# Gated linear attention and a feed-forward layer on one core: chunk ends of three units by another way, clears on VectorE, and a new order of all engines

## The chip, the cores and the metric

The kernel runs on one core of a Trainium2 chip. The metric is device time in microseconds (us) of one execution, as a median over several runs; the profile is one further execution of the same program, with its own time.

## What is computed

Two stages. The first is a gated linear attention, per batch (4) and head (8), over 768 positions with 48 elements a head; the second is a feed-forward layer on its output, 384 to 2048 and back, with a leaky ReLU.

```python
f = 1.0 / (1.0 + np.exp(-f_logit))
state = np.zeros((B, H, D, D), dtype=np.float32)
for t in range(S):
    state = f[:, :, t, :, None] * state + np.einsum('bhd,bhe->bhde', k[:, :, t], v[:, :, t])
    y[:, :, t] = np.einsum('bhd,bhde->bhe', q[:, :, t], state)
...
x = np.ascontiguousarray(attn_out.transpose(0, 2, 1, 3)).reshape(B * S, H * D)
h = x @ w_in
g = np.maximum(0.01 * h, h)
return (g @ w_out).astype(np.float32)
```

Inputs and output are float32; the matmuls take bfloat16.

## The kernel before

**Units.** The positions are cut into chunks of 128. A unit is 256 rows of work (L40). Units 0 to 3 ("paired") are the first two chunks of one batch each; units 4 to 11 are one later chunk (2 to 5) of two batches each. In the words below, the first number is the unit; the second is a half of it (heads 0 to 3 or 4 to 7 of a paired unit, or a chunk or batch), with 2 for both.

**The order** is written out by hand: a string of words (L583), each calling one small function, so that every engine gets its instructions in the order of the words that concern it (the schedule is manual, L53). A word is name_unit_arguments@banks, the banks being PSUM banks of 512 columns. All engines run their own words in sequence; semaphores tie them. SyncE issues all DMAs from one queue, in order, and an issue that has to wait for a buffer holds up those behind it.

**The words of the attention.** Lf, Lk, Lq, Lv load f_logit, k, q, v of a unit (L153; five buffers each). ge and gl (L233, L237) are ScalarE's exponential and logarithm of the gate. cs (L249) sums the logarithms along the chunk on TensorE by a triangular matrix, L264, and for units 4 to 9 also gives the sum over the whole chunk per element, in four narrow matmuls with a column of ones, L267. dec (L273) makes the decays on ScalarE: em (L275), at (L276), and from L267's columns the decay at the chunk's end, end (L281). k and q (L289, work at L293) multiply keys and queries with them; the last number chooses VectorE (0) or GpSimd (1). tk, tq turn both by TensorE in units 0 to 3 (L326), and ck, cq copy the result out of PSUM (VectorE 0, ScalarE 1); xk, xq turn them by a DMA in units 4 to 11 (L346). sc is the scores on TensorE (L362, L369), mk their mask on VectorE (L379, L383), mx their product with the values plus the old state's share (L400), ms the state's share in paired units. xt copies the result to bfloat16 (VectorE 0, ScalarE 1). v (cast_v, L296) casts the values on GpSimd. pt (L464) is the state's new part on TensorE, sf (L481) adds it on VectorE, and sb (state_end, L492) multiplies the state by end and casts it, on GpSimd.

**The words of the feed-forward.** up (L500) makes 256 of the 2048 columns for a unit in six matmuls (L506), pr (L509) is ScalarE's leaky ReLU of them (L511), dn (L513) a quarter of a down-projection in four matmuls (L518), dh a half of the last one by columns (L540). ob and oh copy the output out of PSUM, st and sh store it. WI_0 to WI_4 load w_in in pieces of 384, 384, 768, 768 and 768 KB, WO_0 to WO_3 w_out in pieces of 768 KB; the 768 KB pieces share a ring of three buffers, so that WO_0 needs WI_2's buffer, and WO_3 WO_0's. cw (L186) casts half a piece: cw_0 for w_in, cw_1 for w_out; the last number is VectorE (0), ScalarE (1) or GpSimd (2). up_j_2 and up_j_3 need both halves of WI_2, up_j_4 and 5 those of WI_3, up_j_6 and 7 those of WI_4.

**The filler.** id_n (L202) runs matmuls of 128 n columns on a tile of ones, into a bank that nobody reads then; it computes nothing and lies where TensorE has no work. The order before has 12 of them, 106 blocks of 128 columns, all ahead of unit 2's sums.

**At the start** VectorE clears tiles (L82 to L90) and builds a mask (L114, L116), and L119 clears the eight tiles of the cast states, two on VectorE and six on GpSimd.

## Time and profile before

| | us |
|---|---|
| median of 3 runs | 179.62 (179.17 to 179.93) |
| profiled execution | 179.25 |
| its span, first to last record | 177.4 |

The profile's page gives, for the span: how long each engine was busy and with how many instructions; the span cut into 40 slices; the DMA queues; the chain of work that ended last; and groups of instructions by line, with their busy time, the mean length of one, and the idle time just before them with what ended it. PE is TensorE's matmuls, PEld its weight loads, DVE is VectorE, ACT ScalarE, POOL GpSimd, SP SyncE, and SPq SyncE's issue of DMAs. The granted TensorE clock is a mean of 1.00 over the span. A timeline's row gives start, length, engine, line and operands, and in square brackets the idle time ahead of it. Records of matmuls overlap, since they are pipelined: the time that one costs is read from the distance of two starts.

### The profile page before, as it was taken

To read this page: it belongs to the slowest core of one execution; us is meant where nothing else is said; L and a number is where in the kernel's file an instruction comes from. 1 tells how busy PE (TensorE), PEld (TensorE's weight loads), DVE (VectorE), ACT (ScalarE), POOL (GpSimd) and SP (SyncE) were. 2 spreads that over 40 slices of the span, in tenths; PEclk is the share of its full clock that TensorE was granted. 3 is DMA by queue.
4 is the path that set the end of the run, shared out by engine and by line. 5 is a ranking of instruction groups with operands and counts; after the bars stand their busy time and mean duration, and the time that the engine had idled before them with its cause. 6 is when DMAs were issued, how large, how long until landed. Compare 5 with 4: busy or idle time off the path is not lost.

```text
span 177.4 us, 5625 instructions
## 1 busy us (share of the span) xinstructions
PE 170.6 (96%) x2318; PEld 129.4 (73%) x2318; DVE 83.5 (47%) x164; ACT 114.3 (64%) x236; POOL 64.2 (36%) x137
## 2 busy tenths in 40 slices
PE   7698999999999999999999999999999999999992
...
GB/s 144 283 289 326 358 353 362 364 344 199 221 206 202 222 222 206 185 250 193 234 125 202 182 229 127 235 162 203 172 217 262 0 70 140 89 4 0 48 44 89
DMA packets 106473, 34.44 MB, mean 194 GB/s; under 512 B 100688, under 2 KB 104656, under 8 KB 106448
## 3 DMA queue, kind: packets, MB, share of 16 engines
...
q14 instruction: 7, 0.06, 0.1%
...
## 4 chain that ended last, share of the span: by engine, by line
PE 90%; ACT 3%; DVE 3%; DMA 1%; issue 1%; DVEq 0%
PE ps L506 36%; PE ps L518 35%; PE ps L400 6%; PE ps L369 2%; PE ps L326 2%; DVE qh L293 2%; PE ps L264 2%; PE ps L540 1%; DMA f_raw<-in_f_logit_dram 1%; PE ps L478 1%; DVE wm L379 1%; PE ps L362 1%; PE ps L206 1%; PE ps L473 1%; ACT at L276 1%
## 5 line engine op out<-in xcount | busy, mean ns | idle before, releaser
L511 ACT ACTIVATE gT<-ps 128x512 bf16<-128x512 f32 x96 | 56.2, 620 | 28.7 <-PE ps L506 27.1
L506 PE MATMUL ps<-xT,w_in 128*128 128x256 bf16 x576 | 71.4, 273 | 0.0
L518 PE MATMUL ps<-w_out,gT 128*128 128x384 bf16 x368 | 68.8, 326 | 0.0
L506 PEld LDWEIGHTS <-w_in 128*128 128x128 bf16 x576 | 59.9, 110 | 5.6 <-ACT w_in L198 0.4
L518 PEld LDWEIGHTS <-gT 128*128 128x128 bf16 x368 | 34.2, 98 | 18.7
L495 POOL TENSOR_TENSOR sf<-sf,end 128x192 f32<-128x192 f32 x16 | 9.1, 570 | 40.7 <-DVE sf L490 34.5
L383 DVE TENSOR_TENSOR wm<-ps,ut 128x512 bf16<-128x512 f32 x32 | 19.9, 683 | 8.3 <-PE ps L369 6.5
L564 DVE COPY osb<-ps 128x384 f32<-128x384 f32 x13 | 7.2, 556 | 26.5 <-PE ps L518 20.6
L498 POOL CAST sb<-sf 64x192 bf16<-64x192 f32 x40 | 13.6, 341 | 10.3 <-DVE sf L488 8.0
L293 DVE TENSOR_TENSOR kh<-k_raw,em 128x768 bf16<-128x768 f32 (+1 forms) x10 | 8.5, 853 | 18.6 <-ACT em L275 18.5
L490 DVE TENSOR_TENSOR sf<-sf,ps 64x192 f32<-64x192 f32 x32 | 11.2, 350 | 12.2 <-issue 5.1
L460 ACT CAST xT<-ps 128x384 bf16<-128x384 f32 x14 | 6.9, 513 | 12.7 <-PE ps L400 12.6
L275 ACT ACTIVATE em<-ps 128x384 bf16<-128x384 f32 x24 | 12.1, 503 | 4.2 <-DVE sf L490 2.9
L298 POOL CAST vb<-v_raw 128x384 bf16<-128x384 f32 (+1 forms) x16 | 11.7, 731 | 8.2 <-PE ps L400 5.0
L462 DVE CAST xT<-ps 128x384 bf16<-128x384 f32 x10 | 5.6, 571 | 15.5 <-PE ps L400 15.5
L276 ACT ACTIVATE at<-ps 128x384 bf16<-128x384 f32 x24 | 12.2, 509 | 0.0
L235 ACT ACTIVATE f_raw<-f_raw 128x384 f32<-128x384 f32 (+1 forms) x16 | 10.7, 679 | 1.8 <-DMA f_raw<-in_f_logit_dram 1.8
L379 DVE TENSOR_TENSOR wm<-ps,pair_mask 128x512 bf16<-128x512 f32 x16 | 10.1, 684 | 2.9 <-PE ps L362 2.9
L247 ACT ACTIVATE lf<-f_raw 128x384 bf16<-128x384 f32 (+1 forms) x16 | 10.7, 682 | 0.3
L206 PE MATMUL ps<-warm 128*128 128x512 bf16 (+3 forms) x30 | 9.2, 413 | 1.1 <-DVE warm L82 1.1
L293 POOL TENSOR_TENSOR kh<-k_raw,em 128x384 bf16<-128x384 f32 (+1 forms) x6 | 6.9, 1161 | 8.4 <-DMA q_raw<-in_q_dram 4.4
L293 DVE TENSOR_TENSOR qh<-q_raw,at 128x384 bf16<-128x384 f32 (+1 forms) x11 | 9.3, 857 | 0.0
...
## 6 DMA issues: line engine op xcount, KB each, us to landing
...
ring<-in_moe_w_out_dram SPq DMA_DIRECT2D x4, 768.0 KB, 6.6
...
ring<-in_moe_w_in_dram SPq DMA_DIRECT2D x3, 768.0 KB, 9.1
v_raw<-in_v_dram SPq DMA_DIRECT2D x4, 384.0 KB, 6.4
```

The lines of the kernel that those rows point to most:

```text
L206: nc.tensor.matmul(banks[bank][:, 0:128 * m], warm, warm[:, None, :].to_broadcast([128, m, 128]), start=True, stop=True)
L275: nc.scalar.activation(ems[j % 2][:, a], t[:, 0:H * D], AF.Exp, scale=1.0)
L276: nc.scalar.activation(ats[j % 2][:, a], t[:, 0:H * D], AF.Exp, scale=-1.0)
L293: eng.tensor_mul(heads(j, to[j % NR], a)[:, :, :, 0:D], raw_heads(j, x, a), decays(j, by, a))
L298: nc.gpsimd.tensor_copy(out=heads(j, vb, a), in_=raw_heads(j, "v", a))
L379: nc.vector.tensor_mul(w.rearrange("t (s p) n -> t s p n", s=2), src.rearrange("t (s p n) -> t s p n", s=2, p=2), pair_mask[:, :, None, :] ...
L383: nc.vector.tensor_mul(w, src.rearrange("t (p n) -> t p n", p=P2), ut[:, None, :].to_broadcast([128, P2, 128]))
L490: nc.vector.tensor_add(sf[rows], sf[rows], new)
L498: nc.gpsimd.tensor_copy(out=sb[rows, :, y * D:y * D + D], in_=sf[rows])
L506: nc.tensor.matmul(pm[:, i, :], w_in_of(ff, kk), xTs[j % 3][:, kk].rearrange("t a s -> t (a s)"), start=(kk == 0), stop=(kk == NK - 1))
L511: nc.scalar.activation(gTs[j % 3][:, 2 * g:2 * g + 2, :], pm, AF.Prelu, alpha=0.01)
L518: nc.tensor.matmul(po, gTs[j % 3][:, ff, 128 * a:128 * a + 128], w_out_b[quarter][:, ff % 4, :], start=(ff == 0), stop=(ff == NF - 1))
```

## The change

Four things. Units 5, 7 and 9 (ED) no longer sum whole chunks in L267's matmuls. Instead ScalarE takes, in dec, an exponential of the last 32 rows of the running sums (384 columns) into a new tile, lasts, and the word ed sends its last row to the tile end in two small DMAs from SyncE. VectorE clears all eight tiles of the cast states, and the four tiles end. cast_v can run on ScalarE and state_end on VectorE, by a last number in the word. And the order of all engines is written anew; it has 12 fillers of 112 blocks. The diff, with the orders cut:

```diff
--- before.py
+++ after.py
@@ -58,14 +58,15 @@
         return [const.tile(shape, dtype, name=f"{name}{i}", tag=f"{name}{i}") for i in range(n)]
     NR, NB = 3, 5
-    ED = ()
+    ED = (5, 7, 9)
     raws = {x: tiles(NB, [128, 2, H, D], FP32, x + "_raw") for x in "fkqv"}
     lfs = tiles(NR, [128, 2, H, 64], BF16, "lf")
     khs = tiles(NR, [128, 2, H, 64], BF16, "kh")
     qhs = tiles(NR, [128, 2, H, 64], BF16, "qh")
     ems = tiles(2, [128, 2, H * D], BF16, "em")
-    ats = tiles(2, [128, 2, H * D], FP32 if ED else BF16, "at")
+    ats = tiles(2, [128, 2, H * D], BF16, "at")
     ends = tiles(4, [128, 2, P2], FP32, "end")
+    lasts = tiles(2, [128, 2 * H * D], FP32, "last")
     vbs = tiles(3, [128, 2, H, D], BF16, "vb")
     v2s = tiles(3, [128, 2 * P2, 4, 16], BF16, "v2")
     kTs = tiles(2, [128, 2 * P2, 128], BF16, "kT")
@@ -83,9 +84,6 @@
     for i in range(NR):
         for t in (lfs[i], khs[i], qhs[i]):
             nc.vector.memset(t[:, :, :, D:64], 0.0)
-    if ED:
-        for t in ends:
-            nc.vector.memset(t, 0.0)
     for t in v2s:
         nc.vector.memset(t[:, :, 1:3, :], 0.0)
@@ -116,7 +114,10 @@
         nc.vector.tensor_copy(out=pair_mask[rows, 1, 0:64], in_=bs[rows, rows])
     for b in range(B):
         for t in sbs[b]:
-            (nc.vector if b == 0 else nc.gpsimd).memset(t, 0.0)
+            nc.vector.memset(t, 0.0)
+    if ED:
+        for t in ends:
+            nc.vector.memset(t, 0.0)
     ut = const.tile([128, 128], BF16, tag="ut")
     make_upper_triangular(nc, ut, val=1.0, diag=True)
@@ -277,14 +278,21 @@
         if paired(j):
             nc.scalar.activation(end_of(j)[:, :, 2 * a:2 * a + 2].rearrange("t i p -> t p i"),
                                  t[:, 384:388].rearrange("t (p i) -> t p i", i=2), AF.Exp, scale=-1.0)
-        elif chunk(j, a) < NCH - 1 and j not in ED:
+        elif j in ED:
+            nc.scalar.activation(by_element(j)[C - 32:C, P2 * a:P2 * a + P2],
+                                 t[C - 32:C, 0:H * D].rearrange("t (p y d) -> t p y d", y=2, d=D), AF.Exp, scale=-1.0)
+        elif chunk(j, a) < NCH - 1:
             nc.scalar.activation(end_of(j)[:, a], t[:, H * D:H * D + P2], AF.Exp, scale=-1.0)
+    def by_element(j):
+
+        return lasts[j % 2].rearrange("t (y d g) -> t g y d", y=2, d=D)
+
     def end_dma(j):
+        row = lasts[j % 2][C - 1:C].rearrange("o (y d g) -> o y d g", y=2, d=D)
         for y in range(2):
-            src = ats[j % 2][127:128].rearrange("o a (p y d) -> o y d (a p)", y=2, d=D)[:, y]
-            nc.sync.dma_start(out=end_of(j)[64 * y:64 * y + D].rearrange("d a p -> d (a p)"), in_=src)
+            nc.sync.dma_start(out=end_of(j)[64 * y:64 * y + D].rearrange("d a p -> d (a p)"), in_=row[:, y])
     def scale(x):
         def go(j, a, e):
@@ -293,18 +301,19 @@
             eng.tensor_mul(heads(j, to[j % NR], a)[:, :, :, 0:D], raw_heads(j, x, a), decays(j, by, a))
         return go
-    def cast_v(j, a):
+    def cast_v(j, a, e=0):
         vb, v2 = vbs[j % 3], v2s[j % 3]
-        nc.gpsimd.tensor_copy(out=heads(j, vb, a), in_=raw_heads(j, "v", a))
+        copy = nc.scalar.copy if e else nc.gpsimd.tensor_copy
+        copy(out=heads(j, vb, a), in_=raw_heads(j, "v", a))
         if paired(j):
             p = slice(0, P2) if a == 2 else slice(2 * a, 2 * a + 2)
             src = by_pair(raw(j, "v")).rearrange("t (p j) s d -> t j s p d", j=2)
             dst = v2.rearrange("t (s p) n e -> t n s p e", s=2)
             for i in range(2):
-                nc.gpsimd.tensor_copy(out=dst[:, 3 * i, :, p], in_=src[:, i, :, p, 32 - 32 * i:48 - 32 * i])
+                copy(out=dst[:, 3 * i, :, p], in_=src[:, i, :, p, 32 - 32 * i:48 - 32 * i])
         else:
             a2 = slice(a, a + 1) if a < 2 else slice(0, 2)
-            nc.gpsimd.tensor_copy(out=v2[:, P2 * a2.start:P2 * a2.stop, 0:4:3, :],
+            copy(out=v2[:, P2 * a2.start:P2 * a2.stop, 0:4:3, :],
                                   in_=raw(j, "v")[:, a2].rearrange("t a (p j) d -> t (a p) (j d)", j=2)[:, :, 32:64]
                                   .rearrange("t p (j e) -> t p j e", j=2))
@@ -489,13 +498,14 @@
             else:
                 nc.vector.tensor_add(sf[rows], sf[rows], new)
-    def state_end(j, a):
+    def state_end(j, a, e=0):
+        eng = nc.vector if e else nc.gpsimd
         sf, sb = sfs[batch(j, a)], sbs[batch(j, a)][chunk(j, a) % 2]
         if chunk(j, a) > 0:
-            nc.gpsimd.tensor_mul(sf, sf, end_of(j)[:, a, :, None].to_broadcast([128, P2, D]))
+            eng.tensor_mul(sf, sf, end_of(j)[:, a, :, None].to_broadcast([128, P2, D]))
         for y in range(2):
             rows = slice(64 * y, 64 * y + 64)
-            nc.gpsimd.tensor_copy(out=sb[rows, :, y * D:y * D + D], in_=sf[rows])
+            eng.tensor_copy(out=sb[rows, :, y * D:y * D + D], in_=sf[rows])
     def up(j, g, bank):
         st[j]["pm", g] = bank
@@ -581,69 +591,70 @@
 
     order = """
-    Lf_0_0 Lf_0_1 Lk_0_0 Lk_0_1 Lq_0_0 Lq_0_1 ge_0_0 Lv_0_2 gl_0_0 Lf_1_2 ge_0_1 id_31@6 cs_0_0@0 Lk_1_2 gl_0_1
-    Lq_1_2 cs_0_1@1 dec_0_0 WI_0 k_0_0_0 Lv_1_2 dec_0_1 id_4@6 tk_0_0@2 WI_1 q_0_0_0 k_0_1_1 ck_0_0_1 WI_2
-    id_7@6 tq_0_0@3 q_0_1_0 cq_0_0_0 id_4@6 tk_0_1@4 tq_0_1@5 ck_0_1_1 sc_0_0@6.7 Lf_2_2 v_0_0 cq_0_1_1 mk_0_0_0
-    v_0_1 id_8@2 sc_0_1@0.1 mk_0_0_1 mk_0_1_0 id_7@4 pt_0_2@2.3 WI_3 ge_1_0 mk_0_1_1 ge_1_1 gl_1_0 sf_0_0 id_6@6
-    mx_0_2@4.5 gl_1_1 Lk_2_2 cs_1_0@6 sb_0_0 xt_0_0_1 cs_1_1@7 dec_1_0 sf_0_1 ms_0 k_1_0_1 xt_0_1_0 dec_1_1 WI_4
-    q_1_0_0 k_1_1_1 id_13@1 tk_1_0@0 q_1_1_0 tq_1_0@1 Lq_2_2 cw_0_0_1 ck_1_0_0 sb_0_1 id_3@3 tq_1_1@2 tk_1_1@4
-    cq_1_0_1 up_0_0@3 ck_1_1_0 cq_1_1_1 Lv_2_2 sc_1_0@6.5 v_1_0 pr_0_0 sc_1_1@7.0 mk_1_0_0 cw_0_1_1 v_1_1
-    mk_1_1_0 id_14@2 up_0_1@1 mk_1_1_1 mk_1_0_1 pt_1_2@4.2 pr_0_1 cw_0_3_2 sf_1_0 mx_1_2@3.6 cw_0_2_1 sb_1_0
-    xt_1_0_1 WO_0 id_4@0 up_0_2@7 ge_2_0 ge_2_1 sf_1_1 ms_1 up_0_3@0 pr_0_2 xt_1_1_0 sb_1_1 gl_2_1 up_1_0@5
-    gl_2_0 cw_0_5_1 up_1_2@1 cw_0_4_2 pr_1_0 pr_0_3 WO_1 id_5@3 cs_2_0@4 pr_1_2 cs_2_1@3 dec_2_0 up_1_4@2
-    k_2_0_1 up_1_1@7 dec_2_1 k_2_1_1 up_0_5@6 cw_0_6_0 pr_1_4 tk_2_0@5 pr_1_1 up_0_4@0 cw_0_7_0 pr_0_5 q_2_1_1
-    tk_2_1@1 pr_0_4 up_1_5@4 ck_2_0_0 WO_2 q_2_0_0 up_1_7@3 Lf_3_2 v_2_0 pr_1_5 ck_2_1_0 Lk_3_2 tq_2_0@2 pr_1_7
-    tq_2_1@7 v_2_1 cq_2_0_0 up_0_6@6 cq_2_1_0 sc_2_0@5.0 pr_0_6 cw_1_1_2 sc_2_1@1.4 mk_2_0_0 pt_2_2@3.2 cw_1_0_1
-    ...
-    pr_11_0 up_11_4@3 ob_10_1_0 up_11_1@0 st_10_1 pr_11_4 dn_10_0_2 pr_11_1 up_11_3@7 dn_11_0_0@4 pr_11_3
-    up_11_7@1 dn_11_0_1 pr_11_7 dn_10_0_3 dn_11_0_2 ob_10_0_1 dh_11_1_0@6 st_10_0 dn_11_0_3 oh_11_1_0_1
-    sh_11_1_0 dh_11_1_1 ob_11_0_0 st_11_0 oh_11_1_1_0 sh_11_1_1
+    Lf_0_0 Lf_0_1 Lq_0_1 Lk_0_1 Lk_0_0 Lq_0_0 ge_0_0 Lv_0_2 ge_0_1 Lf_1_2 gl_0_1 Lk_1_2 gl_0_0 id_40@6 cs_0_1@0
+    Lq_1_2 cs_0_0@1 WI_1 dec_0_1 Lv_1_2 k_0_1_0 dec_0_0 q_0_1_0 Lf_2_2 id_16@6 tk_0_1@2 k_0_0_0 ck_0_1_1 id_4@6
+    tq_0_1@3 WI_0 q_0_0_0 cq_0_1_1 id_3@6 tk_0_0@4 ck_0_0_0 id_3@0 tq_0_0@5 sc_0_1@6.7 WI_2 v_0_1_0 cq_0_0_1
+    mk_0_1_0 v_0_0_1 id_5@2 sc_0_0@0.1 mk_0_1_1 id_3@4 pt_0_2@2.3 mk_0_0_0 WI_3 ge_1_0 sf_0_0 gl_1_0 mk_0_0_1
+    ge_1_1 sb_0_0_0 id_16@5 cs_1_0@4 WI_4 gl_1_1 dec_1_0 id_5@6 cs_1_1@5 k_1_0_0 mx_0_2@6.7 dec_1_1 tk_1_0@0
+    q_1_0_0 ms_0 xt_0_0_1 ck_1_0_0 q_1_1_1 tq_1_0@2 xt_0_1_1 sf_0_1 cw_0_1_1 k_1_1_1 cq_1_0_0 id_6@4 tq_1_1@1
+    cq_1_1_0 id_8@6 tk_1_1@4 v_1_0_1 v_1_1_0 sc_1_0@5.0 ck_1_1_1 mk_1_0_0 sb_0_1_0 id_3@3 pt_1_2@6.7 ge_2_1
+    mk_1_0_1 sc_1_1@3.2 ge_2_0 up_0_1@1 sf_1_0 gl_2_1 cw_0_0_2 gl_2_0 cs_2_1@4 mk_1_1_1 pr_0_1 cs_2_0@5 sb_1_0_0
+    mk_1_1_0 dec_2_1 up_0_0@0 mx_1_2@6.2 cw_0_2_1 cw_0_3_0 ms_1 sf_1_1 xt_1_0_1 up_0_3@1 WO_0 pr_0_0 xt_1_1_0
+    sb_1_1_0 Lq_2_2 up_0_2@3 dec_2_0 Lk_2_2 cw_0_4_0 up_1_1@4 pr_0_3 cw_0_5_2 pr_0_2 up_1_3@6 pr_1_1 up_1_0@7
+    pr_1_3 WO_1 up_1_2@0 pr_1_0 Lf_3_2 cw_0_6_0 up_0_4@2 pr_1_2 cw_0_7_0 up_0_5@5 pr_0_4 WO_2 up_0_6@1 pr_0_5
+    cw_1_0_0 cw_1_1_2 up_1_5@3 pr_0_6 up_1_7@4 pr_1_5 q_2_1_0 WO_3 up_1_4@6 pr_1_7 q_2_0_0 Lv_2_2 tq_2_1@7
+    k_2_1_0 k_2_0_1 pr_1_4 Lq_3_2 dn_0_1_0@0 cq_2_1_0 Lf_4_1 tq_2_0@2 tk_2_1@5 Lf_4_0 cq_2_0_1 up_1_6@1 ck_2_1_0
+    Lv_3_2 tk_2_0@3 cw_1_3_1 cw_1_2_2 dn_1_0_0@4 ck_2_0_0 pr_1_6 sc_2_1@6.7 sc_2_0@2.5 Lk_3_2 ge_3_0 mk_2_1_1
+    dn_0_0_0@3 ge_3_1 mk_2_0_0 gl_3_0 dn_1_0_1 gl_3_1 mk_2_1_0 up_0_7@1 Lk_4_0 cw_1_4_1 cw_1_5_2 mk_2_0_1
+    cs_3_0@7 pr_0_7 dn_0_1_1 dec_3_0 cs_3_1@2 Lf_5_1 cw_1_6_0 dn_0_0_1 dec_3_1 cw_1_7_0 dn_1_1_0@6 dn_0_0_2
+    Lf_5_0 v_2_1_1 v_2_0_0 dn_1_1_1 dn_1_0_2 Lk_4_1 q_3_1_0 q_3_0_1 pt_2_2@5.1 mx_2_2@7.2 sf_2_0 Lv_4_1 dn_1_0_3
+    xt_2_0_1 sb_2_0_1 tq_3_1@5 Lv_4_0 ge_4_2 sf_2_1 tq_3_0@7 dn_1_1_2 cq_3_1_0 sb_2_1_0 gl_4_2 ms_2 cq_3_0_0
+    Lf_6_1 dn_1_1_3 ob_1_0_0 v_3_1_1 xt_2_1_0 dn_0_0_3 ob_1_1_1 Lf_6_0 k_3_1_0 k_3_0_1 v_3_0_1 cs_4_0@1 ob_0_0_0
+    cs_4_1@5 dn_0_1_2 dec_4_0 Lq_4_0 tk_3_1@7 dn_0_1_3 dec_4_1 ck_3_1_0 Lq_4_1 tk_3_0@4 Lq_5_1 ge_5_2 ob_0_1_0
+    up_2_0@2 ck_3_0_0 pt_3_2@6.3 pr_2_0 sc_3_0@1.7 sf_3_0 gl_5_2 Lk_5_0 sc_3_1@5.0 k_4_2_1 up_2_1@4 mk_3_1_0
+    Lk_5_1 up_2_5@2 mk_3_0_1 pr_2_1 sb_3_0_0 up_2_2@6 mk_3_1_1 pr_2_5 Lq_5_0 up_2_4@5 v_4_2_0 mk_3_0_0 pr_2_2
+    xk_4 sf_3_1 up_2_3@7 pr_2_4 dn_2_1_0@4 sb_3_1_1 pr_2_3 pt_4_1@0 ge_6_2 cs_5_1@2 cs_5_0@1 sf_4_1 up_2_7@6
+    gl_6_2 sb_4_1_1 mx_3_2@3.5 q_4_2_1 pr_2_7 pt_4_0@7 xt_3_0_0 cs_6_0@0 dec_5_0 ms_3 sf_4_0 dn_2_0_0@6 xt_3_1_0
+    cs_6_1@3 sb_4_0_0 dn_2_1_1 xq_4 dec_5_1 dn_2_0_1 k_5_2_0 st_0_1 up_3_3@7 dec_6_1 q_5_2_1 dn_2_1_2 pr_3_3
+    ...
+    mk_4_0_1 ed_5 dn_3_0_1 mk_4_1_0 Lk_6_1 mk_4_0_0 dn_2_0_3 dn_3_1_0@4 Lk_6_0 up_3_4@0 Lv_6_1 sc_5_2@3.1.2.5
+    ...
+    mx_4_2@5.1 st_1_0 ge_7_2 Lq_6_1 mx_5_2@2.0 gl_7_2 xt_4_1_0 Lf_8_1 xt_4_0_0 ob_2_0_1 pt_5_1@3 pt_5_0@1
+    xt_5_0_1 dn_3_1_2 sf_5_1 Lf_8_0 xt_5_1_1 sf_5_0 up_4_0@5 sb_5_1_0 Lq_6_0 dn_3_0_3 sb_5_0_1 pr_4_0 cs_7_0@6
+    ...
+    st_2_0 dec_8_0 dn_5_0_0@5 q_7_2_0 dec_8_1 dn_5_1_1 dn_4_0_1 dn_5_1_2 k_7_2_1 up_4_6@4 up_5_7@3 pr_4_6 xk_7
+    ...
+    sc_6_2@3.1.7.4 ob_5_1_0 dn_4_0_2 Lk_8_1 mk_6_1_0 st_3_0 dn_5_0_2 mk_6_0_0 st_2_1 Lv_8_1 dn_4_0_3 mk_6_1_1
+    mk_6_0_1 dn_4_1_2 ob_4_0_1 dn_5_0_3 Lk_8_0 mx_6_2@6.7 Lv_8_0 sc_7_2@3.4.1.2 xt_6_0_1 xt_6_1_0 dn_4_1_3
+    ...
+    mk_7_1_0 gl_9_2 Lq_9_0 up_6_4@2 sf_7_0 ob_5_0_1 mx_7_2@6.1 ob_4_1_0 Lq_9_1 pr_6_1 sb_7_0_0 sf_7_1 pr_6_4
+    up_6_5@4 xt_7_0_1 xt_7_1_0 sb_7_1_0 up_6_7@5 k_8_2_0 pr_6_5 up_7_5@0 pr_6_7 v_8_2_0 up_7_6@3 pr_7_5 up_6_0@2
+    ...
+    xk_8 dn_6_1_0@3 pr_7_1 up_7_2@2 dec_9_0 Lf_10_1 k_9_2_1 dn_7_1_0@7 Lf_10_0 q_9_2_0 up_6_6@1 st_5_1 pr_7_2
+    ...
+    ed_9 pt_8_1@5 mk_8_1_1 dn_7_0_3 ob_7_1_1 Lf_11_0 sf_8_1 dn_6_1_1 ob_7_0_1 st_4_1 mk_8_0_0 sb_8_1_0 dn_6_0_1
+    ...
+    q_10_2_0 pr_8_4 sb_9_0_0 up_8_6@4 gl_11_2 st_6_0 mx_9_2@2.3 pr_8_6 xq_10 pr_8_2 cs_11_0@1 xt_9_0_0 cs_11_1@6
+    k_10_2_1 dn_8_1_0@7 dec_11_0 xt_9_1_0 dn_8_0_1 dec_11_1 dn_8_1_1 xk_10 q_11_2_1 up_8_5@4 up_9_4@5 pr_8_5
+    up_8_7@2 pr_9_4 xq_11 k_11_2_1 dn_8_0_2 pr_8_7 up_9_0@3 st_7_0 dn_8_0_3 pr_9_0 xk_11 v_10_2_0 dn_8_1_2
+    ...
+    up_9_7@3 st_8_0 up_9_5@0 pr_9_7 dn_9_0_1 pr_9_5 up_9_6@1 sc_10_2@6.4.3.0 pr_9_6 dn_9_1_1 mk_10_1_0 dn_9_0_2
+    mk_10_0_1 dn_9_1_2 mk_10_1_1 mk_10_0_0 dn_9_0_3 dn_9_1_3 ob_9_0_0 mx_10_2@1.3 ob_9_1_0 sc_11_2@4.0.6.2
+    ...
+    dn_10_1_2 pr_11_6 up_11_3@2 dn_10_1_3 pr_11_3 up_11_5@7 ob_10_1_1 up_11_1@0 pr_11_5 up_11_2@4 pr_11_1
+    up_11_0@5 pr_11_2 dn_10_0_0@3 pr_11_0 up_11_7@6 dn_11_0_0@2 pr_11_7 up_11_4@1 dn_11_0_1 pr_11_4 dn_10_0_1
+    dh_11_1_0@7 dn_10_0_2 oh_11_1_0_1 sh_11_1_0 dn_11_0_2 st_10_1 dn_10_0_3 dn_11_0_3 ob_10_0_1 dh_11_1_1
+    st_10_0 ob_11_0_1 st_11_0 oh_11_1_1_0 sh_11_1_1
```

67 lines of the change are left out of this document (20 added, 47 removed).

## The prediction

> **What bounds the kernel now.** I read the engine row of the page first, then the stretches, then the chain, then SyncE's queue.
>
> ```profile
> PE 170.6 (96%) x2318; PEld 129.4 (73%) x2318; DVE 83.5 (47%) x164; ACT 114.3 (64%) x236; POOL 64.2 (36%) x137
> ```
> TensorE is busy for 96% of the span (its weight loads, PEld, lie beside its matmuls); no other engine comes above 64%. Where are the other 4%, and is the busy time all useful? TensorE in 40 slices of 4.4 us (tenths busy), then two stretches (us; length, then PE, PEld, DVE, ACT and POOL busy, clock, DMA share, GB/s), and the group of the filler:
>
> ```profile
> PE   7698999999999999999999999999999999999992
> ...
> 0.00:17.00 17.00, 13.44 (x209) 7.52 (x210) 14.26 (x35) 11.83 (x27) 11.16 (x36) 1.00 0.92 255
> 17.00:30.00 13.00, 12.92 (x227) 10.24 (x224) 6.98 (x14) 11.52 (x25) 8.82 (x19) 1.00 1.08 357
> ...
> L206 PE MATMUL ps<-warm 128*128 128x512 bf16 (+3 forms) x30 | 9.2, 413 | 1.1 <-DVE warm L82 1.1
> ```
> From 17 us on TensorE has no room. Before that it is idle for 3.6 us, and 9.2 us of its busy time are L206's filler matmuls, which compute nothing. So an order can win only at the start, where the DMA engines are full (share 0.92, then 1.08): TensorE waits there for inputs and weights. Behind the start, time changes only by work taken off TensorE, or by waits put in. The last piece of the chain:
>
> ```profile
> 174.36 0.36 DVE osb L549
> ```
> The new order ends in the same words (dh_11_1_1, oh_11_1_1_0, sh_11_1_1), so these last 3 us stay.
>
> **Chunk ends.** Without the four L267 matmuls:
>
> ```profile
> 50.10 0.33 PE L264 MATMUL ps<-lf,ut 128*128 128x384 bf16 x1
> 50.27 0.24 PE L267 MATMUL ps<-ones_col,lf 128*128 128x1 bf16 x4
> 50.37 0.32 PE L264 MATMUL ps<-lf,ut 128*128 128x384 bf16 x1
> L281 ACT ACTIVATE end<-ps 128x4 f32<-128x4 f32 x12 | 2.4, 199 | 0.0
> L276 ACT ACTIVATE at<-ps 128x384 bf16<-128x384 f32 x24 | 12.2, 509 | 0.0
> ```
> From L264 to L267 it is 0.17 us, and the four L267 take 0.10. Three units with two chunks each save 6 x 0.10 = **0.6 us** of TensorE, all on the path. ScalarE's 32-row exponential isn't in the trace; between the 4-column one (0.20) and the full one (0.51), both over 128 rows, I take 0.51 as its 384 columns are the same: 6 x 0.31 = 1.9 us more on an engine 36% idle, in units whose scores come over 14 us of TensorE work later: nothing on the path. The two DMAs of a unit lie in SyncE's queue behind loads that wait for nothing late, and state_end waits for them. So small a DMA isn't in the trace; between nothing and the slowest load below (9.8 us) I take the quickest there, 5.8. ed_5, ed_7 and ed_9 stand 7 to 9 us of TensorE work ahead of the sb of their unit. Even 9.8 would hold up only GpSimd's five of them and VectorE's sb_5_0_1, behind which unit 6's key product is not urgent; the states are read over 20 us of TensorE work after they are made: nothing. With that cover gone, each us of such a wait would cost one.
>
> **Clearing on VectorE.** VectorE and GpSimd at the start; the last row is the first of VectorE's two qh products, from the chain:
>
> ```profile
> 2.60 0.20 DVE L114 COPY pair_mask<-bu 64x256 bf16<-64x256 bf16 x1
> 3.11 2.37 DVE L114 COPY pair_mask<-bu 64x256 bf16<-64x256 bf16 x1
> 5.90 0.43 DVE L119 MEMSET sb<- 128x192 uint32 x2
> 6.35 0.56 DVE L293 TENSOR_TENSOR kh<-k_raw,em 128x384 bf16<-128x384 f32 x1
> 3.06 2.20 POOL L119 MEMSET sb<- 128x384 bf16 x6
> 6.55 1.13 POOL L293 TENSOR_TENSOR kh<-k_raw,em 128x384 bf16<-128x384 f32 x1 [0.79 <-ACT em L275]
> ...
> 6.86 1.25 DVE qh L293
> ```
> The same copy takes 0.20 and 2.37 us; the second lies beside GpSimd's six clears. With these moved, VectorE loses 2.17 and gains 6 x 0.22 = 1.3, and four clears of 8 columns, between nothing and 0.22 each: it is free 0 to 0.9 us earlier. The other reading, that this copy is slow by itself, is a rival below.
> By the Trainium skill, "SBUF — State Buffer" (the shared port pair), a VectorE operation in a two-port mode and a GpSimd one lock each other out for whole instructions: with it the copy falls to 0.20, without it the sum is that rival's.
> It is worth little: the first product also needs its decays, and in the new order ScalarE does both first exponentials ahead of the first logarithm, so these come one exponential (0.47, the pair at 22.15 below) later; and unit 0's last operand is the sixth load in both orders. I count **0**.
>
> **The new order at the start.** The queue's rows (start and length of the issue), and below each the view of the same issue, whose last number is us to landing:
>
> ```profile
> 10.36 0.49 SPq L157 DMA_DIRECT2D v_raw<-in_v_dram  x1
> v_raw<-in_v_dram SPq DMA_DIRECT2D x1, 384.0 KB, 5.8
> 12.01 0.49 SPq L175 DMA_DIRECT2D ring<-in_moe_w_in_dram  x1
> ring<-in_moe_w_in_dram SPq DMA_DIRECT2D x1, 768.0 KB, 7.8
> 12.54 1.41 SPq L157 DMA_DIRECT2D f_raw<-in_f_logit_dram  x1
> f_raw<-in_f_logit_dram SPq DMA_DIRECT2D x1, 384.0 KB, 8.5
> 16.55 3.57 SPq L175 DMA_DIRECT2D ring<-in_moe_w_in_dram  x1
> ring<-in_moe_w_in_dram SPq DMA_DIRECT2D x1, 768.0 KB, 9.8
> 34.48 0.43 SPq L157 DMA_DIRECT2D q_raw<-in_q_dram  x1
> q_raw<-in_q_dram SPq DMA_DIRECT2D x1, 384.0 KB, 6.2
> ```
> Landings: v of unit 1 at 16.2, the first 768 KB of w_in (WI_2) at 19.8, f of unit 2 at 21.0: in order of issue, 1.2 us for 384 KB. In the new order f of unit 2 moves ahead of WI_2: f lands near 17.4 and WI_2 at 21.0. What needs WI_2 is the third up-projection. TensorE at it now and where unit 3 begins, then prices of parts: ScalarE's gates and casts, and from the chain an up part, two down parts, a mix and a state part:
>
> ```profile
> 21.83 0.82 PE L506 MATMUL ps<-xT,w_in 128*128 128x256 bf16 x6
> 24.98 0.43 PE L206 MATMUL ps<-warm 128*128 128x512 bf16 x2
> 25.25 0.25 PE L256 MATMUL ps<-lf,bu 128*128 128x192 bf16 x1
> 40.02 0.25 PE L256 MATMUL ps<-lf,bu 128*128 128x192 bf16 x1
> 22.15 0.94 ACT L235 ACTIVATE f_raw<-f_raw 128x384 f32<-128x384 f32 x2
> L198 ACT CAST w_in<-ring 128x768 bf16<-128x768 f32 x2 | 1.7, 828 | 0.0
> ...
> 35.02 0.66 PE ps L506 x6
> 35.67 1.30 PE ps L518 x8
> 36.97 0.74 PE ps L400 x61
> ...
> 39.14 0.28 PE ps L400 x12
> ```
> New: 21.0 + 0.83 for ScalarE's cast = 21.9, the same moment as now (21.83). But by then the new order has also done both cs_2 (0.44 each, the distance of the next part from 25.25) and ms_1 (0.28): they fill what is filler and waiting now. Does the rest get there? v of unit 1 at 16.2; ScalarE casts half of it (0.9, an estimate: 0.83 for 768 columns, here 512 in three instructions) and moves kT (0.6, 512 columns, by the 0.51 for 384): 17.7; its four gate instructions of unit 2, 0.47 each, end at 19.6; then cs_2_0 0.44, up_0_0 0.66, mx_1 0.74, ms_1 0.28: 21.7. Just. So it is **1.16 us** ahead, less the 0.07 between 21.83 and 21.9.
>
> From 21.83 to 40.02 the old order does 14 up parts (0.66 each), 6 down parts (0.65), and by the same timeline about 4.1 us of turns, scores, sums and mixes: 17.2 of 18.2 us. Of the 1.0 left, 0.27 is the filler at 24.98; the new order has none behind sc_1_0. I count that and a third of the other gaps, **0.5 us**: with the 0.07 off, 1.6 us by 40 us.
>
> Do the weights and unit 2 follow? WI_4 is the third row pair above: 26.4 now, a load earlier in the new order, so about 25.2; its two casts, 0.83 each at most, end at 26.9 on VectorE, and up_0_6, which needs both, comes at 27.1. SyncE then waits with WO_0 for the casts of WI_2 (21.9) while WI_3 and WI_4 (1.5 MB, over 4 us) are still under way, so the queue doesn't run dry. From WI_4 (26.4) to the last pair of the fence (34.48 + 6.2 = 40.7) thirteen pieces of 384 KB land now, 1.1 us each. At that, WO_0 lands at 27.4, q and k of unit 2 behind it at 28.5 and 29.6; with 0.6 to 0.8 for a cast or product behind them, against uses at 29.9 (the first down part), 29.7 (tq_2_1) and 30.8 (tk_2_1). v of unit 2 moves behind WO_3, which waits for WO_0's casts: twelve pieces behind WI_4, 38.4, with its casts 39.3. pt_2, 18.0 us of parts behind 21.9, comes at 40. That is the tightest. From unit 3 on I only compared the work that TensorE has between a producer and its user: up to down 1.0 us at least (1.2 now), mix to up 1.2 (0.65), sums to scores 14.7 (9.3), scores to mix 2.85 (3.27). All but the last have room.
>
> **Sum.** 0.6 + 1.6 = 2.2 us off the profiled execution's 179.25 (span 177.4): 177.05. The median shown, 179.62, lies 0.37 above it: **177.4**.
>
> **Rivals.**
> *No gain (179.0).* The start stays bound by what comes last: if WO_3 is held as now, v of unit 2 lands when the load behind WO_3 lands now (q_raw, 40.7); with its casts, 41.6, pt_2 waits 1.6 us, and only the 0.6 is left. For it: there are only 0.7 us to spare. Against: WO_0's casts, which release WO_3, come about 3 us earlier. Chance 0.19.
>
> *The copy is slow by itself (178.4).* Then GpSimd's clears were no cause, the 2.37 stay, and six clears come on top: VectorE starts its products 1.3 us later than now, at 7.7. Unit 0's mix would follow by as much; between nothing and all of the 1.3, I let 1.0 reach the third up part. Against: the first copy's 0.20. Chance 0.06.
>
> *The masks become the bound (slower, 181.4).* Scores to mix is the distance that shrinks below the smallest of now: mx_5 2.85, mx_7 2.96, mx_6 and mx_10 3.25 us behind their scores.
>
> ```profile
> L383 DVE TENSOR_TENSOR wm<-ps,ut x32: 679/680/693, 67.7 to 153.2; 128x512 bf16<-128x512 f32 x32
> ```
> Four masks take 2.72 us, and a mix runs 0.35 on the state first (half of its 0.74): VectorE may be 0.5 to 0.9 us late, then each us costs one. The new order gives GpSimd five of the eight large key products (one now). A VectorE product that began alone took 0.56 us, the one behind GpSimd's of 6.55 took 1.25: it ended 0.4 after GpSimd's end at 7.68, as if it had stood still. A large GpSimd product takes 2.3 (twice 1.13); masks that come 1.7 us late behind such a stop cost 1.0 beyond the allowance: at all four mixes 4.0 us. For it: the distances, and the 1.25. Against: no mask went over 693 ns, so the masks themselves don't stop, and in the new list none of VectorE's products stands within 3 us of TensorE work ahead of these four units' masks. The Trainium skill's rule in "SBUF — State Buffer" is this mechanism: two SBUF inputs on VectorE against a GpSimd operation that reads SBUF, and the second to begin waits out the first. The 1.25 agrees. Chance 0.21.
>
> **Chances.** Forecast 0.54, no gain 0.19, slow copy 0.06, masks 0.21. Half a per cent, about what a measurement can tell, is 0.9 us: faster (under 178.7) 0.54 + 0.06 = 0.60, same 0.19, slower 0.21. The forecast's own range is 176.3 (the other 0.5 us of gaps gone too, and the loads 0.6 earlier, half a piece) to 178.3 (half the gain at 40 us lost). For 8 in 10 the range runs from 176.3, with 0.05 below, to 180.6, with 0.15 of the masks' case above.
>
> **What would show it.** Right: no L267 in three units; the second L114 copy near 0.2 us; the third up part near 21.9 with cs_2 done; pt_2 near 40 without a wait; TensorE full from 22 us on. Wrong: idle time on TensorE before pt_2 (v of unit 2), before up_0_6 or the first down part (weights), or before mx_5, mx_6, mx_7, mx_10 (masks). The forecast as a whole fails if loads don't land in order of issue.

## The result, and the profile after

The changed kernel takes 178.59 us (median of 20 runs, 177.76 to 182.12), the kernel before beside it 179.63 (20 runs): a ratio of 0.9936, 95% interval 0.9914 to 0.9959. On the chip of the first experiments it was 178.78 against 179.57, 0.9962 (0.9932 to 0.9992). So it is faster by 0.7 to 1.1 us; the forecast was 2.2. The ratios leave out slow runs (over 1.5% above a kernel's fastest), the medians do not. The profiled execution took 178.35 us, its span is 176.6.

The page's engine row, after:

```profile
PE 170.0 (96%) x2295; PEld 129.7 (73%) x2295; DVE 89.3 (51%) x194; ACT 119.7 (68%) x244; POOL 55.9 (32%) x103
```

The same two stretches as before (length, then PE, PEld, DVE, ACT, POOL busy, clock, DMA share, GB/s):

```profile
0.00:17.00 17.00, 15.72 (x235) 8.85 (x236) 12.98 (x48) 12.96 (x31) 6.26 (x26) 1.00 0.89 242
17.00:30.00 13.00, 11.69 (x202) 10.49 (x202) 7.92 (x15) 11.83 (x28) 6.71 (x14) 1.00 1.05 338
```

TensorE is busy 2.3 us more in the first 17 us and 1.2 us less in the next 13: a hole has come up behind the start. TensorE's timeline shows it, and a second one later:

```profile
21.79 0.35 PE L409 MATMUL ps<-qT,sb 128*32 128x128 bf16 x12
22.82 3.35 PE L516 MATMUL ps<-xT,w_in 128*128 128x256 bf16 x29 [0.68 <-ACT w_in L199]
...
47.67 0.40 PE L335 MATMUL ps<-ident,kh 128*128 128x128 bf16 x4 [0.65 <-DVE kh L301]
```

The third up part starts at 22.82, not 21.9, with everything else done that the forecast wanted done (both cs_2, mx_1, ms_1). At 47.67 the turn of unit 3's k waits. Between and behind them TensorE is full. The last copy, from the chain, against 174.36 before:

```profile
173.29 0.36 DVE osb L559
```

The rows that the clears and the exponential were to change, from VectorE's and ScalarE's, and that of the masks:

```profile
3.12 0.24 DVE L112 COPY pair_mask<-bu 64x256 bf16<-64x256 bf16 x1
...
3.79 1.67 DVE L117 MEMSET sb<- 128x192 uint32 x8
6.62 0.56 DVE L301 TENSOR_TENSOR kh<-k_raw,em 128x384 bf16<-128x384 f32 x1 [1.09 <-ACT em L276]
...
L282 ACT ACTIVATE last<-ps 32x384 f32<-32x384 f32 x6 | 5.2, 872 | 0.1
L392 DVE TENSOR_TENSOR wm<-ps,ut 128x512 bf16<-128x512 f32 x32 | 20.1, 684 | 14.0 <-ACT gT L521 8.0
```

The copy fell from 2.37 to 0.24 us; the first product still waits for its decays. The small exponential takes 0.87 us, above my upper end of 0.51.

### The profile page after: what moved, and what is told of

The parts are those of the page before. It is cut to its first block, busy times and chain, and to the rows that moved or that the text cites. A ratio compares the mean times of both kernels' runs of the same rounds, so it can differ in the third digit from the quotient of the medians.

```text
span 176.6 us, 5545 instructions
## 1 busy us (share of the span) xinstructions
PE 170.0 (96%) x2295; PEld 129.7 (73%) x2295; DVE 89.3 (51%) x194; ACT 119.7 (68%) x244; POOL 55.9 (32%) x103
## 4 chain that ended last, share of the span: by engine, by line
PE 71%; SPq 14%; DMA 10%; POOL 1%; issue 1%; DVE 1%; ACT 0%; DVEq 0%
PE ps L516 30%; PE ps L528 29%; SPq L158 9%; PE ps L409 5%; DMA ring<-in_moe_w_in_dram 4%; DMA k_raw<-in_k_dram 3%; DMA ring<-in_moe_w_out_dram 3%; SPq L162 3%; SPq L176 3%; PE ps L378 3%; PE ps L550 2%; PE ps L265 1%; PE ps L487 1%; POOL w_out L201 1%; ACT w_in L199 0%
## 5 line engine op out<-in xcount | busy, mean ns | idle before, releaser
L516 PE MATMUL ps<-xT,w_in 128*128 128x256 bf16 x576 | 70.0, 273 | 0.7 <-ACT w_in L199 0.7
L516 PEld LDWEIGHTS <-w_in 128*128 128x128 bf16 x576 | 60.8, 110 | 6.2 <-ACT w_in L199 0.9
L307 POOL CAST vb<-v_raw 128x768 bf16<-128x768 f32 (+1 forms) x11 | 8.1, 738 | 31.7 <-DMA v_raw<-in_v_dram 29.1
L505 POOL TENSOR_TENSOR sf<-sf,end 128x192 f32<-128x192 f32 x12 | 6.9, 571 | 31.3 <-DVE sf L499 27.5
L301 POOL TENSOR_TENSOR kh<-k_raw,em 128x768 bf16<-128x768 f32 (+1 forms) x8 | 11.7, 1458 | 12.8 <-DMA k_raw<-in_k_dram 6.7
L276 ACT ACTIVATE em<-ps 128x384 bf16<-128x384 f32 x24 | 12.1, 503 | 2.0 <-PE ps L265 1.2
L469 ACT CAST xT<-ps 128x384 bf16<-128x384 f32 x11 | 5.6, 534 | 11.1 <-PE ps L409 11.0
L508 POOL CAST sb<-sf 64x192 bf16<-64x192 f32 x30 | 11.3, 376 | 3.6 <-DVE sf L497 1.9
L471 DVE CAST xT<-ps 128x384 bf16<-128x384 f32 x13 | 7.2, 567 | 10.1 <-PE ps L409 10.0
L207 PE MATMUL ps<-warm 128*128 128x512 bf16 (+3 forms) x31 | 10.2, 441 | 1.1 <-DVE warm L83 1.1
L572 ACT COPY osb<-ps 128x384 f32<-128x384 f32 x11 | 5.3, 479 | 8.1 <-PE ps L528 8.0
```

What stands on the lines that cost most here:

```text
L276: nc.scalar.activation(ems[j % 2][:, a], t[:, 0:H * D], AF.Exp, scale=1.0)
L301: eng.tensor_mul(heads(j, to[j % NR], a)[:, :, :, 0:D], raw_heads(j, x, a), decays(j, by, a))
L508: eng.tensor_copy(out=sb[rows, :, y * D:y * D + D], in_=sf[rows])
L516: nc.tensor.matmul(pm[:, i, :], w_in_of(ff, kk), xTs[j % 3][:, kk].rearrange("t a s -> t (a s)"), start=(kk == 0), stop=(kk == NK - 1))
```

## The experiments

Twelve runs. **Theory at the outset:** 0.6 us comes from the L267 matmuls, the rest from the order at the start, and what is missing sits in two late transfers (w_in's late 768 KB, 0.9 us; k of unit 3, 0.7). **Rivals:** the chunk ends give nothing; the clears carry the gain; the start is bound by something that a change of loads doesn't move.

| run | edit | median us | ratio to before (95%) |
|---|---|---|---|
| after_again | none | 178.78 | 0.9962 (0.9932 to 0.9992) |
| e1 | before + chunk ends | 182.43 | 1.0173 (1.0153 to 1.0194) |
| e2 | after without chunk ends | 178.65 | 0.9949 (0.9934 to 0.9964) |
| e3 | after, clears on GpSimd | 178.31 | 0.9932 (0.9917 to 0.9947) |
| e4 | after, k of unit 3 earlier | 178.90 | 0.9926 (0.9891 to 0.9960) |
| e5 | after, loads of w_in exchanged | 181.20 | 1.0081 (1.0052 to 1.0110) |
| e6 | e4 and e5 | 180.88 | 1.0102 (1.0059 to 1.0146) |
| e7 | after, f of unit 2 later | 181.30 | 1.0099 (1.0066 to 1.0132) |
| e8 | after + 30 pairs on TensorE | 178.35 | 0.9949 (0.9922 to 0.9976) |
| e9 | e5 + 30 pairs | 178.20 | 0.9912 (0.9880 to 0.9945) |
| e10 | e6 + 30 pairs | 178.09 | 0.9906 (0.9872 to 0.9940) |
| e11 | e4 + 30 pairs | 179.07 | 0.9954 (0.9926 to 0.9982) |

### The parts of the change

> The changed kernel itself, unchanged, on the chip of the three next experiments, so that each can be held against it on the same chip. Both theories: 0.6 % faster than the kernel before (about 1.1 us). In its profile the third up part (the first that needs the late 768 KB of w_in) begins between 22.3 and 23.1 us, and the third unit's k turn waits 0.4 to 1.0 us before 48 us; if these two waits don't come again, they were chance and no cause of the missing gain.

The time came again. The third up part started at 23.01, but TensorE's waits (total, times, longest) name another cause for it, on line 409, and k of unit 3 cost 0.2 only:

```profile
PE ps L409 <- issue: 0.7, 1, 0.7
...
PE ps L335 <- DVE kh L301: 0.2, 1, 0.2
```

"issue" is a wait for nothing that the profile shows. It is taken up under the packets below.

**e1**, the kernel before with

```
-    ED = ()
+    ED = (5, 7, 9)      # and ed_5, ed_7, ed_9 ahead of xk_5, xk_7, xk_9
```

> The kernel before with the chunk ends of units 5, 7 and 9 alone (exponential of the last 32 rows, two small DMAs, the four ends cleared by VectorE); the order is the old one but for the three ed words. My theory (six times four L267 matmuls, 0.10 us each, lie on TensorE's path and go): 0.6 us faster than before, 179.0 against 179.6. Rival, order alone (TensorE fills the 0.6 with waits elsewhere or the small DMAs cost it): 0.0, 179.6, or slower if state_end waits for a DMA on VectorE or GpSimd. The profile gives the landing time of the two small DMAs, which nobody has a row for yet: I take 2 to 6 us.

Neither: 2.9 us slower. Its waits on TensorE, then ScalarE in unit 5, and TensorE's down part behind it:

```profile
PE ps L526 <- ACT gT L519: 2.5, 4, 1.2
...
PE ps L408 <- issue: 0.8, 1, 0.8
```

```profile
63.26 0.48 ACT L276 ACTIVATE em<-ps 128x384 bf16<-128x384 f32 x1
63.63 0.50 ACT L277 ACTIVATE at<-ps 128x384 bf16<-128x384 f32 x1
64.15 0.88 ACT L282 ACTIVATE last<-ps 32x384 f32<-32x384 f32 x1
65.06 0.60 ACT L519 ACTIVATE gT<-ps 128x512 bf16<-128x512 f32 x1
```

```profile
65.71 1.64 PE L526 MATMUL ps<-w_out,gT 128*128 128x384 bf16 x8 [0.34 <-ACT gT L519]
...
95.23 1.47 PE L526 MATMUL ps<-w_out,gT 128*128 128x384 bf16 x8 [1.22 <-ACT gT L519]
...
121.07 2.29 PE L526 MATMUL ps<-w_out,gT 128*128 128x384 bf16 x12 [0.68 <-ACT gT L519]
```

ScalarE runs em, at and last in a row (1.8 us from the first to the end of the last) ahead of a leaky ReLU, the pr word that writes gT, and the down part behind it waits, in all three units (in unit 7 an output copy stands between). None of these waits is in the profile of before or of after. So in the old order the exponentials are on the path: 2.5 us of waits for 0.6 us of matmuls. The profiled run (183.07) is 3.8 slower than before's; 2.5 + 0.8 - 0.6 make 2.7 of it, and 1.1 I can't place. The small DMAs cost nothing that shows: 1.7 us to landing in this run, 2.5 in the changed kernel.

**e2**, the changed kernel with ED = () and no ed words.

> The changed kernel with the chunk ends of units 5, 7 and 9 made as before (24 one-column matmuls back on TensorE, no small DMAs); the order is the new one without the three ed words. My theory: 0.6 us slower than the changed kernel, 179.2. Rival, order alone: the same as the changed kernel, 178.6.

The times can't tell: each interval is half a microsecond wide or more, and they overlap. The traces can, behind 60 us, where both kernels run the same parts without a wait (e2's profiled execution, 180.74, had lost its 2 us before). These are one up part and the last group of matmuls, in after and then in e2:

```profile
60.80 2.78 PE L516 MATMUL ps<-xT,w_in 128*128 128x256 bf16 x24
...
171.72 1.48 PE L550 MATMUL ps<-w_out,gT 128*128 128x192 bf16 x16
```

```profile
62.96 1.25 PE L516 MATMUL ps<-xT,w_in 128*128 128x256 bf16 x10
...
174.28 1.48 PE L550 MATMUL ps<-w_out,gT 128*128 128x192 bf16 x16
```

110.92 against 111.32 us: 0.40 for units 7 and 9, whose sums lie in this stretch. Four chunks of 0.10, as forecast.

**e3**, six sb clears back on GpSimd.

> The changed kernel with six of the eight state clears back on GpSimd. My theory: the second copy of pair_mask stays at 2.4 us or above (it stayed at 3.12 in the changed kernel only if the clears were no cause; in the changed kernel it is 0.24, so it goes back to 2.4 here), VectorE's first product comes later by under 1 us, and the time is the same within 0.3 us, as unit 0's operands come later anyway. Rival, the clears carry the gain: 0.8 to 1.0 us slower than the changed kernel, with the third up part later by as much.

The same time as the changed kernel (178.31). The copy is slow again, and yet the first product is earlier than with the clears on VectorE (6.62):

```profile
3.12 2.38 DVE L112 COPY pair_mask<-bu 64x256 bf16<-64x256 bf16 x1
...
6.44 0.56 DVE L301 TENSOR_TENSOR kh<-k_raw,em 128x384 bf16<-128x384 f32 x1
```

The clears on GpSimd are the cause of the 2.4 us, and the 2.4 us are worth nothing that these runs can tell.

### The loads

**e4** moves one load, **e5** exchanges two, **e6** does both, **e7** puts f of unit 2 back behind the weights:

```
e4   ... cq_2_1_0 Lk_3_2 Lf_4_1 ...        (Lk_3_2 stood behind Lv_3_2)
e5   ... tq_0_1 WI_2 ... sc_0_1 WI_0 ...   (WI_0 and WI_2 exchanged; up_0_0 behind up_0_2)
e7   ... WI_2 Lf_2_2 v_0_1_0 ...           (Lf_2_2 stood ahead of WI_0)
```

> The changed kernel with one load moved: k of unit 3 is issued ahead of the two f loads of unit 4 instead of behind v of unit 3. My theory (two late transfers hold back the gain, this is the second, 0.7 us): the wait before unit 3's k turn goes, and the time is 0.5 to 0.8 us below the changed kernel, about 177.9. Rival (the DMA engines are full there, and another load becomes the late one, f of unit 4 or v of unit 3): 0.0, 178.6, with an equal wait of TensorE between 45 and 60 us.

> The changed kernel with the first two 768 KB loads of w_in exchanged where the late one is needed: the one that held the third up part is issued where the first stood, and the up part that needs the other moves behind the third. My theory (the 0.9 us by which that load landed late is lost gain): the part that waited starts 0.5 to 0.9 us earlier, the time is 0.3 to 0.9 us below the changed kernel, about 178.1. Rival (what binds there is the sum of bytes, not which load comes first): some up part waits as long, 0.0, 178.6.

> The two moves of loads together (k of unit 3 ahead of f of unit 4, and the exchange of the two first loads of w_in). My theory: the gains add, 1.0 to 1.5 us below the changed kernel, about 177.4, which is what I forecast for the change. Rival: the earlier start is eaten up by the next transfers (v of unit 2 at 40 us or k of unit 3 at 47 us), so no more than the better of the two alone.

> The changed kernel with f of unit 2 issued behind the late 768 KB of w_in again, as in the kernel before. My theory (the order of landing is the order of issue, 384 KB take 1.1 to 1.2 us): that weight load lands 1.0 to 1.2 us earlier, near 20.8, but f of unit 2 as much later, and the sums of unit 2 (cs_2), which stand ahead of the up parts on TensorE, wait for it: TensorE stands idle 1 us or more near 20 us, and the time is 0.3 to 1.2 us above the changed kernel. Rival (f's place is worth nothing, the weight load alone sets the pace): 0.5 to 1.0 us below it.

e4 is inconclusive: the interval holds both answers. In its profile unit 3's k turn does not wait any more, but that execution (180.81) had the clock at half for 3.4 us. e5 and e6 went the wrong way for theory and rival alike, by over 2 us. e7 has the wait that I expected, 3.1 us ahead of unit 2's sums, and lost more than I gave it; its clock was at half for 6.8 us, from 20.3 on. In e5 no load was waited for at the place; TensorE's timeline, then its stretches (length, busy, clock, DMA share, GB/s):

```profile
20.48 0.37 PE L409 MATMUL ps<-wm,v 64*32 64x128 bf16 x14
23.22 0.29 PE L409 MATMUL ps<-wm,v 64*32 64x128 bf16 x2 [2.37 <-issue]
23.89 3.36 PE L516 MATMUL ps<-xT,w_in 128*128 128x256 bf16 x19
```

```profile
20.00:22.00 2.00, 0.72 (x54) 1.00 1.02 380
22.00:24.00 2.00, 0.78 (x15) 0.70 1.05 399
24.00:26.00 2.00, 2.00 (x10) 0.50 1.04 393
26.00:28.00 2.00, 2.00 (x19) 0.95 1.12 316
```

TensorE stands still 2.37 us in the middle of a mix, between two matmuls with the same operands, and its clock is at half for 3.4 us, from 22.8 on. All seven runs of e5 had a mean clock of 0.99, and all but two of the fifteen of e6 and e7 had 0.99 or less. By the Trainium skill, "TensorE: Matmul & The Clock Gate" (Part 1), the clock is halved after an idle window of about 3.4 us that runs free of the kernel; here a stand of 2.4 us in 4 us that held 1.5 of work was enough. With stands of about 2 us it went either way: the profiles of e2 and e4 (1.90 each) have the half clock, 3.4 us of it, and those of e3 (1.96) and e6 (1.77) have not. What decides is not shown.

### The packets of TensorE's program

In nine of the first ten traces, those of before and after among them, one place is fixed. The page's DMA part for the changed kernel:

```profile
q8 instruction: 18, 0.29, 0.7%
```

These are 18 packets of 16 KB on a queue of their own, for 2295 pairs of weight load and matmul; between their starts lie 126 pairs on the mean, so about 128 pairs make a packet. I counted TensorE's weight loads, from 0, against these packets in every trace; some of them (us):

| trace | pair 226 starts | second packet | pair 354 starts | wait there | half clock near it, for | profiled execution |
|---|---|---|---|---|---|---|
| before | 17.95 | 20.23 to 21.21 | 22.65 | none | none | 179.25 |
| after | 16.36 | 19.11 to 20.10 | 21.57 | none | none | 178.35 |
| after_again | 16.42 | 20.07 to 21.03 | 22.36 | 0.74 | none | 178.04 |
| e2 | 16.53 | 20.41 to 21.42 | 22.89 | 1.90 | 3.4 | 180.74 |
| e3 | 16.18 | 20.46 to 21.40 | 22.67 | 1.96 | none | 178.34 |
| e5 | 16.38 | 20.93 to 21.89 | 23.44 | 2.37 | 3.4 | 180.92 |
| e6 | 16.40 | 20.32 to 21.37 | 22.81 | 1.77 | none | 178.44 |
| e9 | 14.03 | 16.30 to 17.25 | 20.33 | none | none | 178.25 |

The seven waits that the profile calls "issue" (0.7 to 2.4 us; e1 and e4 have the other two) all stand two or three pairs ahead of pair 354, and that pair started 1.27 to 1.55 us after the second packet's end. In before and after, pair 354 came 1.4 and 1.5 us behind that end, without a wait: just in time. In e7, which waits for its sums, it came later. The packet itself started 2.3 to 4.6 us after pair 226, 128 pairs earlier, while the DMA engines were full. **New theory:** a packet is asked for when TensorE is 128 pairs ahead of needing it, and queues with the loads; between pairs 226 and 354 lie sums, scores and mixes, which are many small matmuls, so the denser the order, the longer TensorE stands there. The last columns show what such a stand costs: e3 and e6 stood about 2 us, kept the clock and took as long as after; e2 and e5 had the half clock and took over 2 us more. The other five runs of e6, with a mean clock of 0.98 or 0.99, took 180.57 to 182.53.

The Trainium skill, "Runtime: NRT & Kernel Launch" (Instruction fetch mechanics), has such blocks of 16 KB, 256 instructions, fetched by a DMA queue of the engine's own, and calls the cost of crossing one mostly hidden. The size agrees with 128 pairs; here TensorE stood up to 2.4 us at the crossing.

The test is to add work: cut the first filler finer, so that the same columns make 30 more pairs and the packet is asked for earlier.

```
-            m = min(n, 4)
+            m = min(n, most)     # most = 1 for id_40, else 4
```

> The changed kernel with one edit: the first filler (5120 columns) is cut into 40 matmuls of 128 columns instead of 10 of 512; the columns and so the time on TensorE at the cold clock stay, and 30 more pairs of weight load and matmul come ahead of everything. New theory, from the first eight runs: TensorE's program comes in packets of 16 KB (128 pairs each) over a DMA queue of its own, a packet is asked for when TensorE is done with the one two before, and shares the full DMA engines with the loads; pair 354 can't start until about 1.3 us after the second packet ends (1.27 to 1.55 in every run that waited there), and that wait of 0.7 to 2.4 us, not the loads alone, takes the gain near 21 to 23 us. With 30 more pairs ahead, that packet is asked for at 14.1 us instead of 16.4, so it ends before 20 and the wait goes; the third up part then starts when the late 768 KB of w_in are cast, 21.9 to 22.8 us; no drop of the clock near 24 us. Time 0.2 to 0.5 us below the changed kernel, about 178.2. Rival (the wait is the loads', the packet only lands with them): the wait before the third up part stays, same time, 178.6.

> The same 30 more pairs, and the first two loads of w_in exchanged as in e5 (which alone made the kernel slower, 181.2). New theory: e5 was slower because TensorE only came sooner to the packet that wasn't there, and stood so long that its clock fell; with the packet early, the exchange gives what it should: third up part at 21.5 or earlier, time 177.4 to 178.0, 3 us below e5. Rival (the exchange itself is bad, as the other up part or the mix waits): 180.5 to 181.5 again.

> The same with k of unit 3 ahead of f of unit 4 as well. New theory: with the start earlier, k of unit 3 is the next late load (0.2 to 0.8 us at 47 us), so 0.2 to 0.8 us below the run before: 176.9 to 177.6. Rival: no difference from the run before, or a wait for another load between 45 and 60 us.

In e9 the second packet ends at 17.25, and pair 354 comes 3.1 us later without a wait. The place where e5 stood, in e9:

```profile
20.87 0.35 PE L410 MATMUL ps<-qT,sb 128*32 128x128 bf16 x12
21.16 6.09 PE L517 MATMUL ps<-xT,w_in 128*128 128x256 bf16 x54
```

e5 to e9, 181.20 to 178.20, differ by those 30 pairs alone: 3.0 us, as expected (on two chips; against before on each, 1.0081 and 0.9912, it is 3.0 too). The time itself, 177.4 to 178.0, was just missed. e10 against e6: 2.8. Against e9, e10 was to gain 0.2 to 0.8 us and didn't (178.09 and 178.20), as its rival had it. In the four kernels with the pairs no "issue" wait is listed and none of 36 runs had a mean clock under 0.996. So the theory holds for what made e5 and e6 slow: the packet, and with it the clock. In the changed kernel 8 of 32 runs (179.65 to 182.12 us) had a mean clock of 0.991 or less; whether the same stand lies behind these isn't shown, as none of them has a trace. For the changed kernel itself it gave less: e8 is 178.35, not told apart from after by its interval, though the profiled run of e8 took 175.92, with no wait on TensorE behind the start at all. Its third up part starts at 21.13:

```profile
21.13 5.10 PE L517 MATMUL ps<-xT,w_in 128*128 128x256 bf16 x45
```

The other eleven runs of e8 lay at 177.79 to 180.04 and have no trace; e11 asked what they waited for.

> The changed kernel with the 30 more pairs ahead and k of unit 3 issued ahead of f of unit 4; the loads of w_in stay as in the changed kernel. The profiled execution with the 30 pairs alone (175.92 us) had no wait on TensorE behind the start, but the other eleven lay at 177.8 to 180.0, so in most of them a transfer between 40 and 60 us must come late. My theory: it is often k of unit 3 (the wait at 47 us in the changed kernel), so 0.3 to 0.8 us below the 30 pairs alone: 177.5 to 178.0; no wait at the second packet of TensorE's program, no clock under 0.996. Rival: the load that is late is another, f of unit 5 (53 us) or v of unit 4: 178.2 to 178.6 as before, and the profile has a wait between 50 and 60 us.

179.07, no gain from k of unit 3: the rival held in that, though the loads that it named (f of unit 5, v of unit 4) are not what TensorE waits for, and its 178.2 to 178.6 was missed. The longest of TensorE's waits in its profile, by time:

```profile
20.75 0.83 PE L517 MATMUL ps<-xT,w_in 128*128 128x256 bf16 x6 [1.02 <-POOL w_in L201]
...
46.17 0.32 PE L266 MATMUL ps<-lf,ut 128*128 128x384 bf16 x1 [0.51 <-ACT lf L249]
58.43 0.32 PE L266 MATMUL ps<-lf,ut 128*128 128x384 bf16 x1 [0.67 <-DVE xT L472]
```

With packet and k out of the way, weights at 21 us and sums of later units wait instead. The last of these waits is in e9 and e10 too (0.98 and 0.61), and its cause can be seen. GpSimd, VectorE and TensorE in e9, then VectorE and GpSimd in after:

```profile
55.33 1.64 POOL L302 TENSOR_TENSOR qh<-q_raw,at 128x768 bf16<-128x768 f32 x1 [1.47 <-DMA q_raw<-in_q_dram]
55.39 1.96 DVE L509 CAST sb<-sf 64x192 bf16<-64x192 f32 x2
57.38 0.59 DVE L472 CAST xT<-ps 128x384 bf16<-128x384 f32 x1
58.02 0.32 PE L266 MATMUL ps<-lf,ut 128*128 128x384 bf16 x1 [0.98 <-DVE xT L472]
```

```profile
56.15 0.52 DVE L508 CAST sb<-sf 64x192 bf16<-64x192 f32 x2
56.92 1.65 POOL L301 TENSOR_TENSOR qh<-q_raw,at 128x768 bf16<-128x768 f32 x1 [2.76 <-DMA q_raw<-in_q_dram]
```

The two casts of a state of unit 4 (sb_4_1_1, on VectorE in the new order) take 0.52 us in after and 1.96 in e9, beside a large product on GpSimd (unit 4's q). In after, after_again and e8 that product begins when VectorE is done with the states of units 3 and 4, or in the last cast; in the nine other traces with the new order it lies beside one of these steps, which takes 1.0 to 1.8 us instead of 0.25 to 0.36. From unit 2's first up part to the eighth behind it TensorE takes 12.0, 12.0 and 12.1 us in those three, 12.1 in e6 and 12.4 to 14.0 in the other eight. In e9, e10 and e11 that is 0.7 to 1.9 us more, of which another wait makes 0.6 in e9. No run here changes this product alone, so what it costs is read from traces, not tested.

As for the late 768 KB, SyncE's queue in after, the chain's row for that load (start, us to landing), and the queue in e8's profiled run:

```profile
12.02 3.48 SPq L176 DMA_DIRECT2D part<-in_moe_w_in_dram  x1
15.55 1.55 SPq L176 DMA_DIRECT2D ring<-in_moe_w_in_dram  x3
```

```profile
15.55 6.37 DMA ring<-in_moe_w_in_dram
```

```profile
12.00 1.82 SPq L176 DMA_DIRECT2D part<-in_moe_w_in_dram  x1
13.86 1.55 SPq L176 DMA_DIRECT2D ring<-in_moe_w_in_dram  x3
```

The issue ahead of it was held 3.48 us in after and 1.82 in e8, both begun at 12.0; so the 768 KB went out at 15.55 and 13.86, landed at 21.9 and 20.2, and the third up part started at 22.82 and 21.13, 1.69 us apart as the issues were. In after the DMA engines' share fell to 0.39 (107 GB/s) from 15.5 to 16.0 us, just behind that hold. In e8 TensorE's mix ended just then too, so it would not have started earlier with the weights there. Why that issue is held longer in one run than in another stays open, and with it what the eleven runs of e8 without a trace waited for.

## Why the prediction was half right

- **L267 gone, 0.6 us:** right, by size too (0.40 for two units of three).
- **ScalarE's exponential, 0.20 to 0.51, off the path:** the term was mis-sized. It took 0.87, so six cost 4.0 us more than the old ends, not 1.9. That it stays off the path is true of the new order only: in e1 the old order pays 2.5 us. "An engine 36% idle" was the wrong row to lean on: what counts is the leaky ReLU queued right behind.
- **Small DMAs hidden:** right; 2.5 us to landing, where I took 5.8.
- **Clears count 0:** right, and so was the cause of the slow copy. Both hold by e3.
- **Third up part at 21.9, 1.16 us ahead:** this step failed. It came at 22.82, with that 1.16 us of work done; so 0.17 of the 1.09 was left. Two things were wrong in it. Landings in steps of 1.2 us from before's leave out that an issue can be held: the 768 KB landed at 21.92, not 21.0. And the packets of TensorE's program were in no term at all; before shows no "issue" wait, as its looser order came to pair 354 just in time. In after itself they cost no wait, in after_again 0.7 us, so there the late landing is what the trace shows for the missing 0.9 us. But e9, with the weights earlier and no wait at the packet, starts its third up part at 21.84, 1.0 us ahead of after, and still takes 178.20: mending the start did not bring the forecast's time, and where the rest goes is only in part seen (the states' casts above).
- **Gaps, 0.5 us by 40 us:** not measured alone. 1.07 at the last copy = 0.6 + 0.17 - 0.65 (k of unit 3) + the rest, which makes 0.95.
- **The tightest spot, pt_2:** well placed, not decisive. v of unit 2 landed near 39.9 instead of 38.4, and pt_2 came at 41.05, 18.2 us behind the third up part (18.0 forecast), without a wait. k of unit 3, five issues further on in the queue, did make TensorE wait; "from unit 3 on I only compared" distances of work, and no landing.
- **Rivals:** the slow copy fell with e3. The masks fell with the trace: 684 ns mean, and no mix waits for a mask behind 23 us. What that rival rests on, a VectorE operation that stands beside a large GpSimd product, did come, in the state's casts of e9 (above) and not in the masks. "No gain" named the right kind of cause, a start bound by what comes last, at another load.
